# Query rounds over all head pairs, kept stacks of keys and queries, and low pieces by VectorE, in an attention and feed-forward kernel

## The chip, the cores and the metric

The kernel runs on one core of one Trainium2 chip. Its engines are TensorE (matmuls; PE in the profile, PEld for its weight loads), VectorE (DVE), ScalarE (ACT), GpSimd (POOL) and SyncE (SP), whose queue issues the DMAs. The metric is the device time of one execution in microseconds; less is better.

## The reference

Attention over 8 batches of 8 heads with 576 queries and keys of width 64, where all scores that lie more than `tau` below the greatest of their row are dropped, and a feed-forward part over the 4608 rows of the result. Cut to what is computed:

```python
def _attn_ref(q, k, v, tau):                       # q, k, v: 8 x 8 x 576 x 64
    scores = scale * np.matmul(q, k.transpose(0, 1, 3, 2))
    thresh = np.max(scores, axis=-1, keepdims=True) - tau
    scores = np.where(scores >= thresh, scores, -1000000000.0)
    attn = np.exp(scores - np.max(scores, axis=-1, keepdims=True))
    attn = attn / (np.sum(attn, axis=-1, keepdims=True) + 1e-09)
    return np.matmul(attn, v)

def _moe_ref(x, w_in, w_out, s, b):                # x: 4608 x 512
    h = x @ w_in                                   # 512 x 2048
    g = s * np.maximum(h, 0.0) ** 2 + b
    return g @ w_out                               # 2048 x 512
```

## The kernel before

Every product runs in half precision on pieces: a 32-bit number is scaled by a power of two and split into a high piece (its 16-bit value) and a low piece (what is left), and products of pieces are added up. Batch 0 alone is done in plain 32-bit form while the weights are loaded and split; batches 1 to 7 are "split".

**Order.** Nothing is written in the order in which it runs. `Plan.add` takes each operation with its engine, what it reads and writes and when it is wanted; `Plan.run` then sets every engine's order from these. Each engine, and SP's queue with the DMAs, takes its instructions in that order, one behind the other.

**Visits.** A visit is one head pair of a batch. In batches 1 to 7 (`WHOLE`) a visit goes over all 576 queries: nine score tiles, four of 128 queries for each head and one with the last 64 queries of both. `make_tiles` sets them, `Visit.load` loads raw q, k (`rq`, `rk`, two buffers) and v (`rv`, one), and `Visit.prepare` makes the pieces. It takes the greatest absolute values (VectorE, L401) and powers of two from them, then scales k and q in place (POOL, L420), casts to the high piece (ScalarE, L422), and subtracts for the low one (POOL, L423). DMAs (L430, L437) stack them for each head: 128 partitions with the high and low queries one above the other, so that one matmul adds two products of pieces. Two such pairs of stacks exist, in the buffers of four weights whose pieces have been moved away (`STACKS_IN`, `moved`). The last queries are copied by POOL (L439) to `qt16`, laid out so that both heads share one matmul. v is scaled (POOL, L448), cast (ScalarE, L458) and its low piece subtracted (POOL, L459), in three buffers.

**A score tile** (`split_tile`): scores on TensorE (L549; four matmuls of 288 columns, the tile of the last queries six) into one of two banks, `s` and `t`; the row maximum on VectorE (L553); threshold and scale on POOL and ScalarE (L555, L557); exponentials on ScalarE (L559); threshold and sum on VectorE (L561); its reciprocal (L564, L566); high piece on ScalarE (L567, L569); low piece on VectorE (L570); a transposing DMA into `ea` or `eb` (L575). When 256 or 320 queries of both heads are there, `with_v` multiplies with v (L585, 14 matmuls for each head, the heads in the two halves of the partitions) and ScalarE copies the result to `xb` (L592).

**Blocks.** 256 rows of the attention's result are a block of the feed-forward part, 512 values each, so all four head pairs must be through; the 64 last queries of four batches make a further one (a tail). `Block.stage` takes a maximum (VectorE, L760), finds powers of two and makes the block's pieces (ScalarE L778, VectorE L782). 16 steps follow, one for each 128 columns of the hidden layer: 12 matmuls `h` (L798), on ScalarE L802, L805, L806, on POOL `gl` (L807), six matmuls `o` (L813). VectorE finishes a block (L827) and SP writes it out (L832). In batch 0 the visits go in two rounds, queries 0 to 255 of all pairs and then the rest; in batches 1 to 7 both blocks of a batch become ready with its last visit.

## Time and profile before

| | |
|---|---|
| median of 3 runs | 1171.56 us (1170.17 to 1172.82) |
| the profiled execution's own time | 1172.21 us |
| its span, first to last instruction | 1170.4 us |
| mean granted TensorE clock | 0.992 |
| busy PE / PEld / DVE / ACT / POOL | 95 / 67 / 75 / 83 / 62% |

How to read it: the span is that of one execution under the hardware profiler. Busy time is the time in which an engine executes something, matmuls' ends are modelled, and instructions of an engine overlap a little, so that from the start of one to the start of the next is often shorter than the duration. The granted clock is a share of TensorE's full 2.4 GHz.

### The profile page before, as it was taken

What the parts mean: (1) busy time and instruction counts of PE and PEld (TensorE: products, weight loads), DVE (VectorE), ACT (ScalarE), POOL (GpSimd) and SP (SyncE); (2) the same over time, 40 slices, a digit from 0 to 9 for tenths busy, and PEclk for the clock granted to TensorE, in tenths of its full rate; (3) what the DMA queues carried; (4) which work ended last, traced back from release to release, by engine and by line L of the source; (5) the groups of instructions that cost most, each with busy time, mean ns of one, the idle gap of its engine ahead of it and who ended that gap; (6) DMA issues with size and microseconds to landing.
All of it is one profiled execution on the core that took longest, in us unless ns stands there. A gap on an engine that the chain in (4) does not pass through costs nothing.

```text
span 1170.4 us, 26444 instructions
## 1 busy us (share of the span) xinstructions
PE 1117.2 (95%) x8826; PEld 781.3 (67%) x8826; DVE 874.8 (75%) x1838; ACT 965.8 (83%) x2301; POOL 721.4 (62%) x1369
## 2 busy tenths in 40 slices
PE   8988888978999999999999999999999999999998
PEld 7766565746666676666676666766776766666665
DVE  5798888798988987888888888787888888730011
ACT  6997888978989889888898888888998989854443
POOL 5565586665767776776675667776777777522200
PEclk9999999998999999999999999999999999999999
DMA  5960168776878777886676777867778786700000
GB/s 163 351 224 2 38 127 165 155 155 146 146 162 153 160 153 149 150 165 132 133 148 139 138 147 145 166 138 144 151 153 172 138 160 127 132 26 1 19 19 18
DMA packets 362232, 155.37 MB, mean 133 GB/s; under 512 B 316016, under 2 KB 340592, under 8 KB 362096
## 3 DMA queue, kind: packets, MB, share of 16 engines
q1 hardware_dynamic: 362096, 153.69, 62.2%
q8 instruction: 69, 1.13, 0.4%
q14 instruction: 67, 0.55, 0.1%
HBM read 46.01 MB, written 9.44 MB: 47 GB/s over the span
## 4 chain that ended last, share of the span: by engine, by line
PE 61%; ACT 12%; DVE 8%; DMA 7%; issue 5%; POOL 4%; SPq 3%; DVEq 0%; POOLq 0%; ACTq 0%
PE h L798 23%; PE o L813 22%; PE pv L585 7%; PE s L549 4%; PE t L549 4%; ACT em L559 2%; ACT en L567 2%; DMA eb<-en 2%; DVE em L561 2%; DVE st L553 2%; DMA rv<-in_v_dram 1%; DMA ea<-in_q_dram 1%; DVE en L570 1%; POOL k L423 1%; ACT iw L802 1%
## 5 line engine op out<-in xcount | busy, mean ns | idle before, releaser
L798 PE MATMUL h<-xp,iw 128*128 128x256 f16 x3456 | 426.4, 273 | 12.9 <-ACT iw L802 8.2
L798 PEld LDWEIGHTS <-iw 128*128 128x128 f16 x3456 | 334.9, 98 | 100.8 <-issue 25.2
L807 POOL TENSOR_TENSOR gl<-iw,gh 128x256 f16<-128x256 f32 x272 | 195.9, 722 | 153.6 <-ACT gh L806 123.8
L813 PE MATMUL o<-ow,gh 128*128 128x512 f16 x864 | 256.9, 379 | 1.6 <-DVE iw L827 1.6
L570 DVE SCALAR_TENSOR_TENSOR en<-em,st,en 128x576 f16<-128x576 f32 x252 | 226.1, 901 | 24.1 <-ACT en L567 21.9
L567 ACT ACTIVATE en<-em,st 128x576 f16<-128x576 f32 x252 | 192.8, 769 | 25.6 <-DVE st L566 21.3
L802 ACT ACTIVATE iw<-h 128x256 f32<-128x256 f32 x288 | 109.0, 378 | 90.1 <-PE h L798 85.5
L813 PE MATMUL o<-ow,gl 128*128 128x512 f16 x432 | 163.7, 379 | 0.0
L555 POOL TENSOR_SCALAR st<-st,wz 128x1 f32<-128x1 f32 x252 | 121.5, 483 | 66.8 <-DVE st L553 48.3
L813 PEld LDWEIGHTS <-gh 128*128 128x128 f16 x1152 | 110.7, 98 | 77.7 <-issue 3.7
L805 ACT ACTIVATE iw<-iw 128x256 f32<-128x256 f32 x288 | 119.7, 416 | 4.0
L806 ACT CAST gh<-iw 128x256 f16<-128x256 f32 x288 | 115.9, 402 | 6.1 <-PE o L813 1.3
L564 POOL TENSOR_SCALAR st<-st 128x1 f32<-128x1 f32 x252 | 70.4, 279 | 81.6 <-DVE em L561 48.0
L561 DVE SCALAR_TENSOR_TENSOR em<-s,st,em 128x576 f32<-128x576 f32 x126 | 102.2, 811 | 21.2 <-ACT em L559 15.7
L549 PEld LDWEIGHTS <-ow 128*128 128x128 f16 x896 | 85.3, 98 | 48.4 <-issue 8.5
L561 DVE SCALAR_TENSOR_TENSOR em<-t,st,em 128x576 f32<-128x576 f32 x126 | 102.4, 813 | 14.4 <-ACT em L559 10.5
L585 PE MATMUL pv<-eb,v 128*64 128x256 f16 (+1 forms) x784 | 107.5, 289 | 5.2 <-DMA eb<-en 5.1
L585 PE MATMUL pv<-ea,v 128*64 128x256 f16 (+1 forms) x784 | 109.2, 290 | 1.3 <-DVE vs L407 1.3
L553 DVE TENSOR_REDUCE st<-s 128x1 f32<-128x576 f32 x126 | 94.5, 750 | 21.0 <-PE s L549 20.6
L585 PEld LDWEIGHTS <-v 128*64 128x64 f16 x1568 | 85.0, 110 | 33.2 <-issue 17.7
L559 ACT ACTIVATE em<-s,st,wz 128x576 f32<-128x576 f32 x126 | 104.0, 825 | 1.2
L559 ACT ACTIVATE em<-t,st,wz 128x576 f32<-128x576 f32 x126 | 104.0, 826 | 1.0
(198 smaller groups left out, 1840.1 us busy)
## 6 DMA issues: line engine op xcount, KB each, us to landing
ow<-k SPq DMA_DIRECT2D x112, 144.0 KB, 2.5
rk<-in_k_dram SPq DMA_DIRECT2D x29, 288.0 KB, 3.2
iw<-in_moe_w_in_dram SPq DMA_DIRECT2D x16, 512.0 KB, 9.4
ow<-in_moe_w_out_dram SPq DMA_DIRECT2D x16, 512.0 KB, 9.2
out_dram<-iw SPq DMA_DIRECT2D x32, 256.0 KB, 2.6
rq<-in_q_dram SPq DMA_DIRECT2D x28, 288.0 KB, 3.5
rv<-in_v_dram SPq DMA_DIRECT2D x56, 128.0 KB, 2.8
ow<-k SPq DMA_DIRECT2D x112, 64.0 KB, 2.2
```

The source lines that it names most:

```text
L549: nc.tensor.matmul(ps[:, hf], stat, kk, start=(n == 0), stop=(n == len(seq) - 1))
L555: pool((260, 263), lambda: nc.gpsimd.tensor_scalar(out=line, in0=top, scalar1=-1.0, scalar2=va.wz[:, 2:3], op0=ALU.mult, op1=ALU.add), [(k ...
L559: act((636, 740), lambda: nc.scalar.activation(out=halves, in_=ps, func=AF.Exp, bias=bias, scale=va.wz[:, 1:2]), [bk, (ks_, 4), (va.kwz, 1 ...
L561: dve((740, 900), lambda: nc.vector.scalar_tensor_tensor(out=halves, in0=ps, scalar=line, in1=halves, op0=ALU.is_ge, op1=ALU.mult, accum_o ...
L567: act((668, 774), lambda: nc.scalar.activation(out=pieces[:, 0:S], in_=ex, func=AF.Copy, scale=unit), [em_k, (ks_, 3)], [en_k], i)
L570: dve2((740, 825), lambda: nc.vector.scalar_tensor_tensor(out=pieces[:, S + T:2 * S + T], in0=ex, scalar=unit, in1=pieces[:, 0:S], op0=ALU ...
L585: nc.tensor.matmul(ps[j * D:(j + 1) * D], hd.v[:, (n + 1) % 5, u * D:(u + 1) * D], lazy[("ea", "eb")[j]][:, n, g.c0:g.c0 + g.n], start=(i ...
L798: nc.tensor.matmul(ps, wi[w][f][:, c * P:(c + 1) * P], x[:, u, c, :], start=(c == 0 and i == 0), stop=(c == NC - 1 and i == 2))
L802: act((357, 473), lambda: nc.scalar.activation(out=g(), in_=ps, func=AF.Relu, scale=H_DOWN), [h, (f"w{(0, 1, 5)[k3]}", "i", 2)], [kg], at)
L805: act((320, 417), lambda: nc.scalar.activation(out=g(), in_=g(), func=AF.Square), [kg], [kg], at)
L807: do((712, 735) if not self.last else (340, 425), lambda: eng.tensor_tensor(out=lo, in0=g(), in1=hi, op=ALU.subtract), [kg, f"gh{k3}"], [f ...
L813: nc.tensor.matmul(bank["o"][:, t, :], a[:, ts_], w, start=(f == 0 and i == 0), stop=(f == NF - 1 and i == 2))
```

## The change

Each of the batches 1 to 7 is now done like batch 0: first queries 0 to 255 of all four head pairs, four score tiles each, then queries 256 to 511 and the last 64, five tiles each. A pair's preparation is done once in a batch and what it makes is kept for the second round. So four visits have buffers of their own: eight stacks instead of four (one in the memory of the plain batch's `qs`, seven in weights' buffers, whose pieces are moved), eight buffers for v instead of three (six in weights' buffers), four of the small tables. The stacks now hold three things, the queries in full and both pieces of the keys, so that `qt16` goes. The tile of the last queries takes eight matmuls with 64 columns of the array each, alternating between the heads, which lie in the two halves of the partitions. High pieces are cast by ScalarE with the scale as part of the instruction, low pieces made by VectorE in one instruction (multiply by the scale, subtract the high piece); POOL's seven instructions of that kind go. A visit's stacks are made by four DMAs of 216 KB instead of eight of 144 and 64 KB. The columns of `ea` and `eb` are used in turn by even and odd pairs.

```diff
-WHOLE = range(1, 8)
...
-STACKS_IN = 6
+STACKS_IN = (None, 0, 7, 8, 9, 10, 11, 12)
+VALUES_IN = (1, 2, 3, 4, 5, 6)
+SPARES = (1, 2, 4, 5, 6, 3)
...
-            self.n, self.wz, self.kwz = i % 2, wz[i % 3], f"wz{i % 3}"
-            self.kpc = [("piece", self.n, c) for c in range(4)]
-            self.kqt = [(f"qt16_{self.n}", j) for j in range(2)]
+            self.n, self.m, self.wz, self.kwz = i % 4, i % 2, wz[i % 4], f"wz{i % 4}"
+            self.kpc = [("piece", self.m, c) for c in range(4)]
...
+        def stack(self, j):
+
+            return lazy["y", 2 * self.n + j]
...
             for c, (t, key) in enumerate(raw):
-                up = x[:, 9 + c:10 + c]
-                pool((722, 742), lambda t=t, up=up: nc.gpsimd.tensor_scalar(
-                    out=t, in0=t, scalar1=up, scalar2=1.0, op0=ALU.mult, op1=ALU.mult), [key, (kx, 3)], [key], at)
-                act((612, 717), lambda c=c, t=t: nc.scalar.copy(out=self.piece(2 * c), in_=t), [key], [self.kpc[2 * c]], at)
-                pool((1385, 1420), lambda c=c, t=t: nc.gpsimd.tensor_tensor(
-                    out=self.piece(2 * c + 1), in0=t, in1=self.piece(2 * c), op=ALU.subtract),
-                    [key, self.kpc[2 * c]], [self.kpc[2 * c + 1]], at)
+                up, hi, lo = x[:, 9 + c:10 + c], 1 - c, 2 + c
+                act((612, 717), lambda hi=hi, t=t, up=up: nc.scalar.activation(
+                    out=self.piece(hi), in_=t, func=AF.Copy, scale=up), [key, (kx, 3)], [self.kpc[hi]], at)
+                dve2((658, 743), lambda hi=hi, lo=lo, t=t, up=up: nc.vector.scalar_tensor_tensor(
+                    out=self.piece(lo), in0=t, scalar=up, in1=self.piece(hi), op0=ALU.mult, op1=ALU.subtract),
+                    [key, (kx, 3), self.kpc[hi]], [self.kpc[lo]], at)
             for j in range(2):
                 own = slice(j * D, (j + 1) * D)
                 for u in range(2):
-                    to = slice(u * D, (u + 1) * D)
-                    dma(144, lambda j=j, own=own, to=to: nc.sync.dma_start(
...
-                pool((330, 330), lambda j=j, own=own: nc.gpsimd.tensor_copy(
...
+                    to, turn = slice(u * D, (u + 1) * D), slice(4 * m, 4 * m + 3) if not u else slice(4 * m + 3, 4 * m, -1)
+                    dma(216, lambda j=j, own=own, to=to, turn=turn: nc.sync.dma_start(
+                        out=self.stack(j)[to], in_=lazy["k"][own, turn]), self.kpc[u:u + 3], [("y", 2 * n + j, u)], at)
...
-            pool((775, 796), lambda: nc.gpsimd.tensor_scalar(
-                out=flat, in0=flat, scalar1=x[:, 11:12], scalar2=1.0, op0=ALU.mult, op1=ALU.mult),
...
-                pool((775, 797), lambda t=t, own=own, other=other, j=j: nc.gpsimd.tensor_tensor(
-                    out=t[:, :, other], in0=rv[:, j], in1=t[:, :, own], op=ALU.subtract), kr + keys, keys, at)
...
+                dve2((400, 485), lambda hd=hd, own=own, other=other, j=j, up=up: nc.vector.scalar_tensor_tensor(
+                    out=hd.values()[:, :, other], in0=rv[:, j], scalar=up, in1=hd.values()[:, :, own], op0=ALU.mult, op1=ALU.subtract),
...
         def scores():
             for hf in range(2):
-                c, j = slice(hf * HS, (hf + 1) * HS), ti.slot
-                if j is None:
-                    seq = [(qt16[va.n][:, u], va.piece(w)[:, c]) for u, w in ((0, 0), (0, 1), (1, 0))]
-                else:
-                    seq = [(va.queries_of(j)[:, ti.n * P:(ti.n + 1) * P], va.keys_of(j, w)[:, c]) for w in range(2)]
-                for n, (stat, kk) in enumerate(seq):
-                    nc.tensor.matmul(ps[:, hf], stat, kk, start=(n == 0), stop=(n == len(seq) - 1))
+                c = slice(hf * HS, (hf + 1) * HS)
+                for w in (1, 2):
+                    for j in js:
+                        y = va.stack(j)
+                        to, q = (ps[:, hf], slice(ti.n * P, (ti.n + 1) * P)) if ti.slot is not None else (
+                            ps[j * T:(j + 1) * T, hf], slice(M, S))
+                        nc.tensor.matmul(to, y[:, 0, q], y[:, w, c], start=(w == 1), stop=(w == 2))
...
-    visits = []
-    for bi in range(B):
-        if bi in WHOLE:
-            visits += [(bi, p_, 0, NQ, True) for p_ in range(NP)]
-        for u in range(0 if bi in WHOLE else 2):
-            visits += [(bi, p_, 2 * u, 2 * u + 2, (bi > 0 and p_ < NP // 2) == (u == 0)) for p_ in range(NP)]
+    visits = [(bi, p_, 2 * u, 2 * u + 2, u == 1) for bi in range(B) for u in range(2) for p_ in range(NP)]
...
+        u, at = us[0], (0, M - NB + T)[pair % 2]
...
-        for j, n in [(0, 0), (0, 1), (0, 2), (1, 0), (1, 1), (0, 3), (None, 4), (1, 2), (1, 3)]:
+        for j, n in [(0, 0), (1, 0), (None, 2), (0, 1), (1, 1)]:
+            if j is None and not tail:
+                continue
```

On VectorE, around the staging of the third block, which is the first block of batch 1. L553, L561, L566 and L570 are the instructions of a score tile (`st` its statistics, `en` its pieces), L760 the maximum over a block, `x`, L401 that over raw `rk`, `rq` or `rv`, L412 a power of two for it, L827 the end of a block. Before:

```order
L553 TENSOR_REDUCE st_74<-t 128x1
L570 SCALAR_TENSOR_TENSOR en_77<-em_80,st_71,en_77 128x576
L566 RECIPROCAL st_73<-st_73 128x1
L412 TENSOR_SCALAR vs_103<-vs_103 128x3
L827 SCALAR_TENSOR_TENSOR iw_528<-o,power_96,iw_454 128x512
L570 SCALAR_TENSOR_TENSOR en_75<-em_78,st_72,en_75 128x576
L570 SCALAR_TENSOR_TENSOR en_76<-em_79,st_73,en_76 128x576
L760 TENSOR_REDUCE norm_84<-x_113 128x1
L561 SCALAR_TENSOR_TENSOR em_80,st_74<-t,st_74,em_80 128x576
L764 TENSOR_TENSOR nsq_86<-norm_84 128x1
```

and with the change, where the numbers of the lines are four to five lower (L549 is the maximum, L557 the threshold, L562 the reciprocal, L566 the low piece, L406 the maximum over raw values, L756 that over the block):

```order
L549 TENSOR_REDUCE st_70<-t 128x1
L566 SCALAR_TENSOR_TENSOR en_77<-em_80,st_74,en_77 128x576
L406 TENSOR_REDUCE vm_83<-rq 128x1
L566 SCALAR_TENSOR_TENSOR en_75<-em_78,st_69,en_75 128x576
L557 SCALAR_TENSOR_TENSOR em_79,st_70<-t,st_70,em_79 128x576
L549 TENSOR_REDUCE st_71<-s 128x1
L756 TENSOR_REDUCE norm_84<-x_113 128x1
L549 TENSOR_REDUCE st_72<-t 128x1
L760 TENSOR_TENSOR nsq_86<-norm_84 128x1
L557 SCALAR_TENSOR_TENSOR em_80,st_71<-s,st_71,em_80 128x576
L562 RECIPROCAL st_70<-st_70 128x1
```

The maximum over the block stood behind the low piece of the 35th of batch 1's 36 tiles; now it stands behind that of the 19th, and reductions over raw values of later visits stand near it.

On POOL, at the preparation of the first visit of batch 2. L555 and L564 are the small instructions of a tile. Before:

```order
L415 TENSOR_TENSOR vs_103<-vs_103,spread 128x3
L420 TENSOR_SCALAR rk<-rk,vs_103 128x576
L564 TENSOR_SCALAR st_73<-st_73 128x1
L420 TENSOR_SCALAR rq<-rq,vs_103 128x576
L423 TENSOR_TENSOR k<-rk,k 128x576
L423 TENSOR_TENSOR k<-rq,k 128x576
L555 TENSOR_SCALAR st_74<-st_74,wz_92 128x1
L442 TENSOR_SCALAR wz_90<-vs_103 128x1
L445 TENSOR_SCALAR wz_90<-vs_103,spread 128x1
L448 TENSOR_SCALAR rv<-rv,vs_103 128x640
```

and with the change (L551, L560 the small ones of a tile, L803 the feed-forward's `gl`, L420 and L436 to L442 a visit's small tables, L714, L764 and L767 a block's powers of two), at the same preparation:

```order
L560 TENSOR_SCALAR st_72<-st_72 128x1
L803 TENSOR_TENSOR gl_120<-iw_393,gh_117 128x256
L714 TENSOR_SCALAR power_94<-power_94 128x1
L551 TENSOR_SCALAR st_73<-st_73,wz_91 128x1
L420 TENSOR_TENSOR vs_102<-vs_102,spread 128x3
L439 TENSOR_SCALAR wz_90<-vs_102,spread 128x1
L551 TENSOR_SCALAR st_74<-st_74,wz_91 128x1
L764 TENSOR_SCALAR power_94<-power_94 128x1
L767 TENSOR_TENSOR power_94<-power_94 128x1
L560 TENSOR_SCALAR st_73<-st_73 128x1
```

The wide instructions on `rk`, `rq`, `rv` and `k`, which stood ahead of a tile's small ones, are gone; only the visit's tables are left.

On VectorE, in the first round of batch 2 with the change (L427 makes a low piece of q or k, L452 one of v, whose buffers now lie in those of the weights, `ow`):

```order
L562 RECIPROCAL st_74<-st_74 128x1
L427 SCALAR_TENSOR_TENSOR k<-rk,vs_103,k 128x576
L549 TENSOR_REDUCE st_70<-t 128x1
L566 SCALAR_TENSOR_TENSOR en_77<-em_80,st_74,en_77 128x576
L557 SCALAR_TENSOR_TENSOR em_78,st_69<-s,st_69,em_78 128x576
L452 SCALAR_TENSOR_TENSOR ow_304<-rv,vs_103,ow_304 128x5x64
L452 SCALAR_TENSOR_TENSOR ow_376<-rv,vs_103,ow_376 128x5x64
L562 RECIPROCAL st_69<-st_69 128x1
L557 SCALAR_TENSOR_TENSOR em_79,st_70<-t,st_70,em_79 128x576
L427 SCALAR_TENSOR_TENSOR k<-rq,vs_103,k 128x576
```

Before, the rows between the tiles of the same place read:

```order
L570 SCALAR_TENSOR_TENSOR en_75<-em_78,st_69,en_75 128x576
L570 SCALAR_TENSOR_TENSOR en_76<-em_79,st_70,en_76 128x576
L561 SCALAR_TENSOR_TENSOR em_80,st_71<-s,st_71,em_80 128x576
L401 TENSOR_REDUCE vm_82<-rk 128x1
L553 TENSOR_REDUCE st_72<-t 128x1
L760 TENSOR_REDUCE norm_85<-x_111 128x1
L566 RECIPROCAL st_71<-st_71 128x1
L553 TENSOR_REDUCE st_73<-s 128x1
L561 SCALAR_TENSOR_TENSOR em_78,st_72<-t,st_72,em_78 128x576
L401 TENSOR_REDUCE vm_82<-rq 128x1
```

Four low pieces of a visit have come in between the tiles' instructions.

## Rows read from the trace of the kernel before

**Rows 1.** The page: busy time and share of the span of TensorE.
```profile
PE 1117.2 (95%) x8826; PEld 781.3 (67%) x8826; DVE 874.8 (75%) x1838; ACT 965.8 (83%) x2301; POOL 721.4 (62%) x1369
```
**Rows 2.** Busy us (instructions) of PE, PEld, DVE, ACT, POOL; clock, DMA share, GB/s.
```profile
300.00:360.00 60.00, 57.49 (x464) 39.45 (x462) 49.84 (x102) 52.33 (x129) 41.43 (x79) 1.00 0.77 153
...
480.00:540.00 60.00, 59.26 (x478) 41.64 (x478) 52.84 (x113) 53.48 (x133) 39.83 (x77) 1.00 0.77 150
...
900.00:960.00 60.00, 60.00 (x473) 41.47 (x473) 53.15 (x112) 54.07 (x134) 44.05 (x78) 1.00 0.78 152
...
1040.00:1080.00 40.00, 39.48 (x277) 26.94 (x276) 3.28 (x4) 20.21 (x50) 10.48 (x17) 1.00 0.04 14
```
**Rows 3.** The same in stretches of 10 us.
```profile
140.00:150.00 10.00, 8.06 (x53) 4.88 (x52) 5.57 (x10) 4.83 (x13) 9.09 (x16) 1.00 0.61 158
...
160.00:170.00 10.00, 8.13 (x55) 5.21 (x54) 9.38 (x19) 8.75 (x20) 9.22 (x17) 1.00 0.56 114
...
250.00:260.00 10.00, 5.89 (x50) 3.23 (x47) 10.00 (x21) 7.98 (x18) 7.34 (x11) 1.00 0.78 147
260.00:270.00 10.00, 4.24 (x18) 2.49 (x19) 8.24 (x18) 4.50 (x9) 6.09 (x18) 0.52 0.83 163
270.00:280.00 10.00, 10.00 (x76) 6.74 (x75) 7.79 (x14) 7.80 (x21) 3.83 (x9) 0.80 0.65 154
```
**Rows 4.** The chain of waits from 245 to 285 us: start us, us, what.
```profile
258.37 1.78 POOL k L423
...
261.49 2.01 DMA ow<-k
...
267.08 1.30 DVE xp L782
```
**Rows 5.** Timeline of PE: start us, us, line, out<-in, partitions x columns.
```profile
562.62 0.65 PE L549 MATMUL s<-ow 128*128 128x288 f16 x4
563.11 0.59 PE L813 MATMUL o<-ow,gh 128*128 128x512 f16 x2
...
909.78 0.65 PE L549 MATMUL s<-ow 128*128 128x288 f16 x4
910.37 0.32 PE L585 MATMUL pv<-ea,v 128*64 128x320 f16 x1
...
912.16 0.30 PE L585 MATMUL pv<-eb,v 128*64 128x320 f16 x1
912.39 1.48 PE L798 MATMUL h<-xp,iw 128*128 128x256 f16 x12
```
**Rows 6.** Timeline of DVE, five instructions without a gap.
```profile
561.16 0.82 DVE L561 SCALAR_TENSOR_TENSOR em<-s,st,em 128x576 f32<-128x576 f32 x1 [1.19 <-ACT em L559]
...
561.90 0.81 DVE L570 SCALAR_TENSOR_TENSOR en<-em,st,en 128x576 f16<-128x576 f32 x1
562.63 0.75 DVE L553 TENSOR_REDUCE st<-t 128x1 f32<-128x576 f32 x1
563.31 0.76 DVE L553 TENSOR_REDUCE st<-s 128x1 f32<-128x576 f32 x1
563.99 0.15 DVE L566 RECIPROCAL st<-st 128x1 f32<-128x1 f32 x1
```
**Rows 7.** Groups of instructions: busy us, mean ns of one, idle before.
```profile
L570 DVE SCALAR_TENSOR_TENSOR en<-em,st,en 128x576 f16<-128x576 f32 x252 | 226.1, 901 | 24.1 <-ACT en L567 21.9 <-DMA eb<-en 0.4
...
L459 POOL TENSOR_TENSOR v<-rv,v 128x320 f16<-128x320 f32 x56 | 45.0, 804 | 16.5 <-ACT v L458 15.3
...
L827 DVE SCALAR_TENSOR_TENSOR iw<-o,power,iw 128x512 f32<-128x512 f32 (+1 forms) x40 | 28.9, 743 | 12.6 <-PE o L813 12.6
...
L782 DVE SCALAR_TENSOR_TENSOR xp<-x,power,xp 128x1024 f16<-128x1024 f32 x16 | 21.6, 1348 | 38.7 <-ACT xp L778 38.5
...
L760 DVE TENSOR_REDUCE norm<-x 128x1 f32<-128x1024 f32 x16 | 19.4, 1211 | 5.0 <-ACT x L592 5.0
L439 POOL COPY qt<-k 64x128 f16<-64x128 f16 x56 | 19.2, 343 | 2.0
```

More of the change, by code (lines that the diff above doesn't have):

```diff
@@ L685, in weight_scales @@
         pool((1800, 1800), back, ["wpower", "s_", "b"], ["wback"], at + 1)
-    moved = [(STACKS_IN + n, 1) for n in range(4)]
+    moved = [(f, 1) for f in STACKS_IN if f is not None]
     def pieces_of_weights(f, at):
@@ L900, in make_tiles @@
             if j is not None:
[L901 to L903 removed]
+                ti.heads, ti.parts = [(A, Bh)[j]], [(("ea", "eb")[j], at + n * P, fl)]
             else:
[L905 removed]
+                ti.heads, ti.parts = [A, Bh], [("ea", NB, slice(0, T)), ("eb", NB, slice(T, P))]
             tiles.append(ti)
+        tiles[-1].end = [group]
@@ L907, in make_tiles @@
         if pair == NP - 1:
-            blocks = tiles[-1].blocks
-            blocks += [("full", bi, u) for u in us]
-            if t1 == 4 and bi % 4 == 3:
-                blocks.insert(0 if bi == B - 1 else len(blocks), ("tail", bi // 4, 0))
+            tiles[-1].blocks = [("full", bi, u)]
+            if u and bi % 4 == 3:
+                tiles[-1].blocks.insert(0 if bi == B - 1 else 1, ("tail", bi // 4, 0))
         return tiles
     pairs = [Plain(0, p_) for p_ in range(NP)]
-    heads = [Head(2 * vi + j, vis[0], 2 * vis[1] + j) for vi, vis in enumerate(visits) for j in range(2)]
```

110 lines of the change are left out of this document (53 added, 57 removed).

## Prediction

> **What bounds the kernel now.** I read the busy times first. TensorE is at work for 1117 of 1170 us [rows 1], and the 10 us and 60 us stretches show where it is not. In the steady part it leaves 2.5 us of 60 idle at 300, 0.7 at 480 and none at 900, with VectorE at 50 to 53 of 60 [rows 2]. At the end, where only the feed-forward part is left, 277 matmuls take 40 us; a step is 12 + 6 of them, so a step costs 2.60 us [rows 2]. So the span is TensorE's own work plus the holes in it. One hole is large: from 250 to 280 us TensorE is busy 5.9, 4.2 and 10.0 us of the slices, and the granted clock reads 0.52 and 0.80 in the last two, which is most of the time at 1.2 GHz instead of 2.4 after the engine had stood still [rows 3]. The chain of waits tells why. Both blocks of batch 0 are used up, those of batch 1 become ready only when the whole batch is through, and just then the next visit is prepared: POOL's subtractions, the stack DMA, then VectorE's low piece of the staged block, for which the h matmuls wait [rows 4]. The prologue has smaller gaps, 1.9 us at 140 and 1.9 at 160 [rows 3].
>
> I write "tile" for 128 queries of one head, or the 64 last queries of both, against 576 keys; each batch from 1 to 7 has 36, before and after. The sum is made against the profiled execution's own 1172.2 us (span 1170.4, the rest around it); the median of the runs, 1171.6, lies 0.65 below it, and I subtract that at the end.
>
> **1. Rounds: blocks become ready half a batch earlier.** After the change the first block of a batch is complete after 16 tiles instead of 36. In the order, VectorE takes the maximum of the third block (the first of batch 1) behind 35 tiles' low pieces before, and behind 19 now, when TensorE has 30 of the 32 steps of batch 0 behind it. Two steps (5.2 us) and the score tiles between them then cover the staging. So the hole should be filled. Its price: idle 4.1 us, then 10 - 4.24 x 0.52 = 7.8, then 10 x 0.20 = 2.0, together 13.9; an ordinary stretch at 300 has 2.5 of 60 idle anyway, 1.2 of 30, so **-12.7 us** is the gain, with 0 as the other end, if the hole only moves. The end of the program keeps its form: TensorE alone at 2.60 us a step.
>
> **2. The tile of the last queries.** 28 times six matmuls of 288 columns become eight, each 64 columns of the array wide, in pairs that write the two halves of the partitions. A score tile of four matmuls takes 0.49 us from its start to the next matmul (562.62 to 563.11) [rows 5], so 0.12 each, six 0.73. If a pair runs side by side, eight cost four, 0.49. The product with v shows that pairs do: its 14 pairs, 320 columns wide, take 2.02 us (910.37 to 912.39), 0.144 a pair, where one after the other they would take twice that [rows 5]. But the same rows show what the change of form costs. The score tile ahead of such a group takes 0.59 instead of 0.49, and its last pair 0.23 instead of 0.13: 0.10 us going in, 0.10 coming out. So a tile costs 0.49 + 0.20 = 0.69 against 0.73, and 28 of them give **-1.1 us**; the ends are -6.7 (no cost of the change of form) and +6.7 (pairs one after the other). I take the middle since these rows have the same form.
> The Trainium skill, "TensorEngine Tiling (Array Packing)", section "Key Properties", says that changing the tiling mode drains the engine. The 0.10 us on either side agrees; without that rule the term would be -6.7, with it -1.1.
>
> **3. Work leaves POOL.** Seven groups of POOL go, from the low pieces of v, 45.0 us, to the copies of the last queries, 19.2: 218 us in all, 7.8 per visit [rows 7] (the first and the last of the seven stand there). POOL is 62% busy and mostly off the path, so most of this is worth nothing. In two places it ends last: in the hole (already counted), and ahead of the first split tile at 147 us. The gaps of TensorE there are 1.9 and 1.9 us [rows 3]; I take half, **-2 us**, with 0 and -3.8 as ends. The stacks' eight DMAs per visit become four of 216 KB each; they are issued on SP's queue, ahead of the transposes, and the queue gets shorter. The visit's own loads are the same. The high pieces on ScalarE are the same two casts with a scale in them. I cost all this at nothing: its cover is that a stack is now asked for once in a batch and stays.
>
> **4. VectorE takes the low pieces.** Per visit two 576 wide ones of the form of L570, and two 320 wide. L570 runs 0.81 us undisturbed, with the next instruction 0.73 behind it, and 0.90 in the mean [rows 6, 7], so one occupies 0.73 to 0.82; 320 columns by proportion 0.41 to 0.46. I take 0.80 and 0.45, an estimate from those rows: 2.5 us a visit, 70 us in all on an engine that is busy 875.
> What matters is where. A tile costs VectorE 0.74 (L561) + 0.82 (L570) + 0.68 (L553) + 0.15 (L566) = 2.39 us [rows 6]. A visit's preparation costs three reductions at 0.7, small ones some 0.4 and the new 2.5: 5.0. A block costs 1.2 + 1.35 to stage and twice 0.74 to finish, 4.0 [rows 7]. A first round has 16 tiles and, if nothing moved, all four preparations: 38.2 + 20.0 + 4.0 = 62.2 us. TensorE has in it 16 steps, 16 tiles at 0.49 and four products of 1.6 (2.02 by 256/320): 41.6 + 7.8 + 6.5 = 55.9. The second round is the other way about: 51.8 against 60.4. So a first round would be bound by VectorE by 6.3 us, 44 us over seven batches. The order moves part of the preparation into the second round before. Counting its rows at these prices in stretches of nine tiles, VectorE has more to do than TensorE in eight stretches from tile 18 on: by 4.4, 3.1, 2.5, 3.8 and 3.0 us in five, under 1 in three, 18.7 in all, and each is followed by one with 2 to 8 us to spare (without the change the same count gives 13.2, of which 6.7 is the hole). In-order queues with two score banks can make up part of that. So the bounds are 0 and 44; I take a third of 18.7, **+6 us**, nearer to 0, because VectorE runs at 53.15 of 60 at 900 us with TensorE never idle [rows 2]. Behind a late VectorE instruction wait the score matmuls, since their bank is not free, and behind those the feed-forward matmuls in TensorE's queue.
> The Trainium skill, "SBUF — State Buffer", section "Who interferes with whom", says that a VectorE instruction with two SBUF inputs and a GpSimd instruction that reads SBUF exclude each other for their whole length. L570's mean of 0.90 against 0.81 agrees. By it the 30% that POOL loses would give VectorE some 30% of 252 x 0.09, 7 us, over the program, and the term would be nearer to 4 than to 6.
>
> **Sum.** 1172.2 - 12.7 - 1.1 - 2 + 6 = 1162.4; less 0.65, **1162 us**.
>
> **Rivals.**
> *VectorE becomes the bound.* Place: the first rounds of batches 2 to 5, and the two batches before, where all three engines are even. From tile 18 to 90 the counts give VectorE 232 us and TensorE 236. If VectorE cannot go above 53.15 of 60, the most that any row here shows, those 232 take 262, while TensorE with its usual 2% idle would take 240: +22, and 8 more in the later batches (3.8 + 3.0 + 0.6 + 0.8), so +30: 1172.2 - 15.8 + 30 - 0.65 = **1186**. It decides from +15.8 on. For it speaks that the order stages each block with only one or two steps left, so there is little stock; against it that feed-forward steps need no VectorE.
> *All of it works.* VectorE's surplus is absorbed, the pairs cost no change of form, the prologue's gaps close: 1172.2 - 12.7 - 6.7 - 3.8 - 0.65 = **1148**. The row at 900 us speaks for the first, the rows of the product with v against the second.
> *The hole only moves.* Four visits are prepared in the first 16 tiles of batch 1, so that block may be late and batch 0's steps run out as before: 1172.2 - 1.1 - 2 + 6 - 0.65 = **1174**. Against it stand the two steps in hand.
>
> **How the numbers follow.** Forecast 0.48 (1155 to 1169), all of it works 0.24, VectorE the bound 0.18, the hole moves 0.10. A measurement of this kernel tells 0.2% (2.3 us) from no change. Faster: all but the edge of the forecast, and the second rival, 0.70; same 0.08, from the edge of the forecast and half of the last rival; slower 0.22. The range goes from 1147, the second rival, to 1181, most of the way to the first; below and above lie about 0.2.
>
> **What would show it.** Right: no stretch with a granted clock under 0.9 between 240 and 290 us; the third block staged near 200 us; the tail tile's eight matmuls within 0.7 us; VectorE at 54 or more of 60 around 280 to 420 us with TensorE at 58 or more. Wrong: TensorE waiting for score banks that VectorE frees, in the first halves of the batches, by more than 15 us in all; or feed-forward matmuls waiting for staged pieces again.

## The result, and the profile after

The changed kernel takes 1136.74 us in the median (1134.79 to 1137.64, 4 runs) beside 1172.19 for the kernel before in the same session: a ratio of 0.969 (95% interval 0.967 to 0.972), 35.4 us less. The forecast was 1162 with a range of 1147 to 1181: faster was right, but the time lies 10 us below the range and the gain is three and a half times the one worked out. One run of a kernel below, e8, went at a granted clock of 0.851 and took 1274.0 us; its time in the table is the median of the other three.

The span and the busy line of the page after (beside [rows 1]):

```profile
span 1135.8 us, 26196 instructions
PE 1106.7 (97%) x8882; PEld 770.5 (68%) x8882; DVE 917.3 (81%) x1950; ACT 967.7 (85%) x2301; POOL 546.5 (48%) x1117
```

POOL is busy 175 us less than before, VectorE 42.5 us more, and TensorE stands still for 29 us of the span instead of 53. The place is found with four long stretches: ahead of the old hole, around it, and the two halves of the steady part. Columns: stretch and its length, busy us and instructions of PE, PEld, DVE, ACT, POOL, then granted clock, DMA share, GB/s. Before:

```profile
0.00:240.00 240.00, 215.25 (x1770) 160.29 (x1771) 196.62 (x420) 205.56 (x436) 151.14 (x304) 0.99 0.59 153
240.00:300.00 60.00, 49.08 (x375) 32.70 (x374) 52.86 (x110) 49.16 (x117) 37.45 (x72) 0.89 0.74 150
300.00:660.00 360.00, 350.95 (x2812) 243.39 (x2810) 301.07 (x629) 318.56 (x781) 252.78 (x473) 1.00 0.76 149
660.00:1040.00 380.00, 377.14 (x3023) 261.64 (x3021) 307.97 (x654) 333.70 (x824) 257.38 (x486) 1.00 0.71 141
```

and after:

```profile
0.00:240.00 240.00, 222.70 (x1833) 164.66 (x1834) 200.94 (x434) 209.48 (x442) 131.67 (x274) 1.00 0.60 157
240.00:300.00 60.00, 59.52 (x487) 40.76 (x485) 56.04 (x121) 54.29 (x134) 32.77 (x64) 1.00 0.84 162
300.00:660.00 360.00, 354.55 (x2866) 243.80 (x2865) 319.04 (x677) 322.85 (x793) 179.92 (x371) 1.00 0.73 147
660.00:1040.00 380.00, 379.49 (x3091) 261.63 (x3090) 324.54 (x686) 337.68 (x828) 187.24 (x383) 1.00 0.74 142
```

From such rows I work out what a stretch **loses**: the time in which PE is idle, plus PE's busy time times what the clock lacks. The hole's stretch loses 60 - 49.08 + 49.08 x 0.11 = 16.3 us before and 0.5 after. In the same way 0 to 240 us goes from 26.9 to 17.3 (the clock's two digits make that uncertain by 1 us; added up from rows of 10 us, the first two losses before are 26.1 and 15.0), and 300 to 1040 from 11.9 to 6.0. Together 55.1 against 23.7: 31.4 of the 35.4 us. Of the other 4 the tail tile has 1.1 (below); the rest I can't place. Over all kernels below, the profiled execution's time less its loss is 1114 to 1121 us, so the losses carry the times to within some 4 us.

The five 10 us stretches that answer [rows 3], three of them shown, are full, where before they had 8.1, 8.1, 5.9, 4.2 and 10.0 us busy, and the 60 us stretches that answer [rows 2] hold a surprise:

```profile
140.00:150.00 10.00, 10.00 (x67) 6.21 (x65) 5.71 (x10) 7.68 (x16) 6.42 (x13) 1.00 0.58 137
160.00:170.00 10.00, 10.00 (x63) 5.81 (x61) 8.02 (x15) 8.40 (x19) 5.28 (x11) 1.00 0.93 210
260.00:270.00 10.00, 10.00 (x86) 6.86 (x85) 8.65 (x20) 9.33 (x23) 6.25 (x14) 1.00 0.55 110
...
300.00:360.00 60.00, 58.76 (x484) 40.76 (x483) 55.34 (x119) 54.74 (x134) 32.82 (x64) 1.00 0.80 159
660.00:720.00 60.00, 60.00 (x502) 41.82 (x502) 56.91 (x120) 53.96 (x132) 31.21 (x64) 1.00 0.90 183
1040.00:1080.00 40.00, 39.55 (x272) 26.35 (x271) 5.83 (x14) 20.57 (x50) 12.83 (x23) 1.00 0.04 14
```

At 660 us VectorE is busy 56.91 of 60 while TensorE never stops; before, the highest was 53.15 [rows 2], which the prediction took for a possible ceiling. At the end, from 1040 us on, TensorE is as full as before.

### The profile page after: what moved, and what is told of

Its sections match the earlier page's. It is cut to its first block, busy times and chain, and to the rows that moved or that the text cites. A ratio compares the mean times of both kernels' runs of the same rounds, so it can differ in the third digit from the quotient of the medians.

```text
span 1135.8 us, 26196 instructions
## 1 busy us (share of the span) xinstructions
PE 1106.7 (97%) x8882; PEld 770.5 (68%) x8882; DVE 917.3 (81%) x1950; ACT 967.7 (85%) x2301; POOL 546.5 (48%) x1117
## 4 chain that ended last, share of the span: by engine, by line
PE 74%; ACT 8%; DVE 6%; issue 3%; DMA 3%; POOL 1%; SPq 1%; DVEq 0%; ACTq 0%; POOLq 0%
PE h L794 27%; PE o L809 27%; PE pv L581 7%; PE s L545 4%; PE t L545 4%; ACT en L563 2%; ACT em L555 1%; DVE em L557 1%; DMA eb<-en 1%; PE pv L517 1%; DVE st L549 1%; ACT iw L798 1%; DMA ea<-en 1%; PE t L504 1%; PE s L481 1%
## 5 line engine op out<-in xcount | busy, mean ns | idle before, releaser
L794 PE MATMUL h<-xp,iw 128*128 128x256 f16 x3456 | 424.8, 273 | 10.2 <-ACT iw L798 9.4
L803 POOL TENSOR_TENSOR gl<-iw,gh 128x256 f16<-128x256 f32 x272 | 202.3, 744 | 208.4 <-issue 82.6
L566 DVE SCALAR_TENSOR_TENSOR en<-em,st,en 128x576 f16<-128x576 f32 x252 | 209.6, 836 | 21.4 <-ACT en L563 20.1
L809 PE MATMUL o<-ow,gh 128*128 128x512 f16 x648 | 192.9, 379 | 0.7 <-DVE iw L823 0.7
L551 POOL TENSOR_SCALAR st<-st,wz 128x1 f32<-128x1 f32 x252 | 121.5, 483 | 111.3 <-DVE st L549 68.0
L560 POOL TENSOR_SCALAR st<-st 128x1 f32<-128x1 f32 x252 | 86.1, 342 | 144.1 <-DVE em L557 76.2
L809 PE MATMUL o<-iw,gh 128*128 128x512 f16 x504 | 150.0, 379 | 0.2 <-DVE iw L823 0.2
L809 PE MATMUL o<-ow,gl 128*128 128x512 f16 x324 | 122.8, 379 | 0.0
L557 DVE SCALAR_TENSOR_TENSOR em<-t,st,em 128x576 f32<-128x576 f32 x126 | 102.3, 812 | 19.9 <-ACT em L555 13.6
L545 PEld LDWEIGHTS <-ow 128*128 128x128 f16 (+1 forms) x980 | 85.1, 100 | 47.8 <-issue 13.5
L557 DVE SCALAR_TENSOR_TENSOR em<-s,st,em 128x576 f32<-128x576 f32 x126 | 102.3, 812 | 13.0 <-ACT em L555 8.9
L555 ACT ACTIVATE em<-s,st,wz 128x576 f32<-128x576 f32 x126 | 103.9, 824 | 1.1
L555 ACT ACTIVATE em<-t,st,wz 128x576 f32<-128x576 f32 x126 | 103.8, 824 | 1.1
L553 ACT ACTIVATE st<-st,wz 128x1 f32<-128x1 f32 x252 | 72.9, 290 | 36.3 <-DVE st L549 34.8
L809 PEld LDWEIGHTS <-gl 128*128 128x128 f16 x576 | 56.3, 98 | 68.0
L549 DVE TENSOR_REDUCE st<-t 128x1 f32<-128x576 f32 x126 | 94.4, 749 | 8.8 <-PE t L545 7.2
```

The lines of the kernel that those rows point to most:

```text
L545: nc.tensor.matmul(to, y[:, 0, q], y[:, w, c], start=(w == 1), stop=(w == 2))
L551: pool((260, 263), lambda: nc.gpsimd.tensor_scalar(out=line, in0=top, scalar1=-1.0, scalar2=va.wz[:, 2:3], op0=ALU.mult, op1=ALU.add), [(k ...
L555: act((636, 740), lambda: nc.scalar.activation(out=halves, in_=ps, func=AF.Exp, bias=bias, scale=va.wz[:, 1:2]), [bk, (ks_, 4), (va.kwz, 1 ...
L557: dve((740, 900), lambda: nc.vector.scalar_tensor_tensor(out=halves, in0=ps, scalar=line, in1=halves, op0=ALU.is_ge, op1=ALU.mult, accum_o ...
L566: dve2((740, 825), lambda: nc.vector.scalar_tensor_tensor(out=pieces[:, S + T:2 * S + T], in0=ex, scalar=unit, in1=pieces[:, 0:S], op0=ALU ...
L794: nc.tensor.matmul(ps, wi[w][f][:, c * P:(c + 1) * P], x[:, u, c, :], start=(c == 0 and i == 0), stop=(c == NC - 1 and i == 2))
```

## The experiments

Eighteen kernels ran. The kernel before took 1170.8 to 1173.5 us in their sessions. "Order" in the table is a number that the planner assumes for the time from one engine to another, 150 ns in both kernels; 152 changes no instruction, only the order.

| kernel | rounds in 1 to 7 | low pieces of q, k, v | order | us | loses 0:300 | 300:1040 |
|---|---|---|---|---|---|---|
| before | no | POOL | 150 | 1172.2 | 43.2 | 11.9 |
| e7_before_152 | no | POOL | 152 | 1178.7 | 42.4 | 14.0 |
| e4_before_dve | no | VectorE | 150 | 1168.7 | 40.5 | 9.6 |
| e9_neither | no | POOL | 150 | 1155.4 | 34.0 | 4.5 |
| e14_neither_152 | no | POOL | 152 | 1166.7 | 37.1 | 10.1 |
| e1_whole | no | VectorE | 150 | 1160.6 | 37.6 | 6.9 |
| e15_whole_152 | no | VectorE | 152 | 1155.7 | 32.7 | 8.8 |
| e2_pool | yes | POOL | 150 | 1148.0 | 20.3 | 9.7 |
| e16_pool_152 | yes | POOL | 152 | 1145.6 | 19.7 | 9.9 |
| after | yes | VectorE | 150 | 1136.7 | 17.8 | 6.0 |
| e8_after_152 | yes | VectorE | 152 | 1138.2 | 17.7 | 6.1 |

**How much an order alone does.** One number of the planner, in both kernels:

```diff
-    HANDOVER = 150
+    HANDOVER = 152
```

> The kernel before with the same number of the planner moved from 150 to 152: the same instructions in a slightly different order. If the order's chance is small: within 3 us of 1172. If the kernel before had a bad order by chance: 10 us or more faster.

> The changed kernel with one number of the planner moved from 150 to 152: the same instructions in a slightly different order. It measures how much of any difference is chance of the order. If the order's chance is small: within 3 us of 1137. If the gain of 35 us is largely chance: 10 us or more away.

Measured 1178.66 (ratio to before 1.0048, 1.0031 to 1.0066; before took 1173.23 in that session) and 1138.19 (0.9705, 0.9689 to 0.9721; two expectations below take 1139.0, +2.3, the median of all four runs). With the pairs that follow, the same work in two orders differs by +5.4, +1.5, +11.3, -4.9, -2.3 and -2.1 us, some 6 us in the root mean square. The runs of one kernel agree to about 2 us; it is the order that is uncertain. So a comparison of two kernels whose order differs is good to no better than 6 us, one of two means over both orders to some 4, and what follows rests on both orders wherever it can.

**Rounds and VectorE's pieces, each without the other.** e1 sets a pair's two rounds back to back, nearly as one visit does in the kernel before (the first block of a batch is asked for with the 31st of its 36 tiles, there with the 36th); e2 has POOL scale and subtract again; e9 does both.

```diff
 e1: visits
+ [... batch 0 as it is] + [(bi, p_, 2 * u, 2 * u + 2, u == 1)
+     for bi in range(1, B) for p_ in range(NP) for u in range(2)]
 e2: prepare, q and k (v alike)
+ pool(..., nc.gpsimd.tensor_scalar(out=t, in0=t, scalar1=up, scalar2=1.0, ...))
+ act(..., nc.scalar.copy(out=self.piece(hi), in_=t))
+ pool(..., nc.gpsimd.tensor_tensor(out=self.piece(lo), in0=t, in1=self.piece(hi), op=ALU.subtract))
```

> The changed kernel with its two rounds of a head pair back to back in batches 1 to 7, so that both blocks of a batch become ready with the last pair again; stacks, pieces and the tile of the last queries stay as changed. Theory A (three parts: blocks ready earlier some 15 us, the prologue some 10, the rest of the program some 10 by the work that left POOL): only the first part goes, about 1152 us, with the hole and a low granted clock back near 250 to 280 us. Theory B (the rounds bring nearly all): 1165 us or more, with TensorE behind in the later batches too. Theory C (blocks ready earlier matter little): about 1137.

> The changed kernel with scaling and low pieces of q, k and v on POOL as before (rounds, kept stacks, last queries in halves stay). Theory A: the rest of the program loses its some 10 us, about 1147, with POOL near 700 us busy and VectorE near 850. Theory of the prediction (VectorE's load costs about 6 us): faster than the changed kernel, about 1131. Theory B (the rounds bring nearly all): 1137 within 3.

> The changed kernel with both of its main parts taken back: a pair's two rounds stand back to back in batches 1 to 7, and POOL again scales and subtracts; the kept stacks, four copies, tail tile and their order stay. Rounds alone taken back gave 1160.6, POOL alone 1147.9. Theory A, the two parts add up: 1136.7 + 23.9 + 11.2 = 1172 us. Theory B, VectorE's relief is worth as little without rounds as in the kernel before (4.8): 1165 us. Either way TensorE's work done by 220 us should be some 8 us ahead of the kernel before if the prologue's gain belongs to what is left.

> The run without rounds and with POOL's pieces (1155.4 us), with the planner's assumed time from engine to engine at 152 ns instead of 150: the same work in another order, which moved the kernel before by +5.3 and the changed one by +2.3 us. Theory A, that rounds and VectorE's pieces help each other is real: 1152 to 1159 us, and below the run with VectorE at 152. Theory B, the 1155.4 was a lucky order: 1160 us or more.

> The run without rounds and with VectorE's pieces (1160.6 us) at 152 ns. Theory A, without rounds VectorE's pieces cost time: 1158 to 1165 us, at least 3 above the same with POOL. Theory B, that was the order: at or below the same with POOL.

> The run with rounds and POOL's pieces (1147.9 us) at 152 ns. Theory A, with rounds VectorE's pieces are worth 11 us: 1147 to 1152 us, at least 8 above the changed kernel at 152 ns (1139.0). Theory B, part of the 11 was the order: 1140 to 1145 us.

Beside what was expected: e1 (1160.6) lies between its A and B, e2 (1148.0) fits A, e9 (1155.4) lies under both of its theories, e14 and e15 fit B, e16 (1145.6) ends just above B's range. At 150 the table looks like a strong interplay: VectorE's pieces gain 11.2 us with rounds and cost 5.2 without. The second order takes that back: there they gain 7.4 with rounds and 11.0 without, since e9's 1155.4 was a lucky order (e14: 1166.7). What stands in the means of both orders: rounds bring 14.3 us with POOL's pieces and 20.7 with VectorE's; VectorE's pieces bring 9.3 with rounds, and 2.9 without, which 4 us of uncertainty can't tell from nothing; and what is left of the change when both are taken back brings 14.4 (1175.4 to 1161.1).

The hole is the one place where all orders agree. Rows of 240 to 300 us, of e1, e15, e9, e2 and e16 in turn:

```profile
240.00:300.00 60.00, 46.97 (x361) 31.59 (x360) 55.16 (x122) 50.06 (x115) 28.91 (x61) 0.87 0.80 160
240.00:300.00 60.00, 54.44 (x421) 36.20 (x420) 55.09 (x120) 52.42 (x128) 30.55 (x67) 0.97 0.73 156
240.00:300.00 60.00, 52.75 (x426) 35.38 (x424) 55.28 (x116) 52.19 (x125) 40.51 (x78) 0.97 0.73 157
240.00:300.00 60.00, 57.77 (x458) 38.22 (x457) 50.33 (x112) 54.93 (x138) 43.54 (x85) 1.00 0.88 168
240.00:300.00 60.00, 58.39 (x487) 40.02 (x482) 52.23 (x113) 54.97 (x138) 43.22 (x81) 1.00 0.85 152
```

In the first three TensorE is idle for 5.6 to 13 us and the granted clock falls; with rounds, in the last two, it is idle for 1.6 to 2.2 us at the full clock, whoever makes the pieces. Up to 300 us all kernels of the table without rounds lose 33 to 43 us, those with rounds in all batches 18 to 20.

**Rounds in batches 0 and 1 only.**

```diff
+ [... for bi in range(2) for u in range(2) for p_ in range(NP)] +
+ [... for bi in range(2, B) for p_ in range(NP) for u in range(2)]
```

> The changed kernel with rounds in batches 0 and 1 only; in batches 2 to 7 a pair's rounds stand back to back. Rounds in all batches are worth 23.9 us (1160.6 without). Theory A, most of that is the hole at 250 to 280 us, which rounds in batch 1 alone fill, and the rest (some 8 us) comes from blocks that are ready in time later: 1143 to 1148 us, no granted clock below 0.9 from 240 to 300 us. Theory B, all of it is the hole: 1137 us. Theory C, the hole moves to the next batch, where the blocks again come late: 1152 us or more, with a gap of over 5 us between 300 and 420 us.

Measured 1152.97 (0.9833, 0.9817 to 0.9848). In time it fits C, by the trace A: from 240 to 300 us TensorE is busy 59.34 at a clock of 1.00, and no gap comes in the next batch. The time was lost earlier, 25.5 us by 240 us instead of 17.3, with one wait of 3.6 us for a stack's DMA in 120 to 180 us; from 300 to 1040 us it loses 10.2, 3 more than e1. So rounds in batch 1 are enough for the hole, and they fill it rather than move it. Whether later rounds bring anything can't be told from one order.

**VectorE's load.** e4 is the kernel before with the pieces made by VectorE as in the change. e3 is the changed kernel in which VectorE makes the low pieces of q and k twice, with the same result.

```diff
 e4, prepare of the kernel before: the change's own lines for act(...) and dve2(...) in place of POOL's
 e3, prepare of the changed kernel
                 dve2((658, 743), lambda ...: nc.vector.scalar_tensor_tensor(out=self.piece(lo), ...
+                dve2((658, 743), lambda ...: nc.vector.scalar_tensor_tensor(out=self.piece(lo), ...
```

> The kernel before, with only the low pieces of q, k and v moved to VectorE and their scaling into ScalarE's casts. Theory A: some 10 us faster than before, about 1162, the hole at 250 to 280 us stays or shrinks by POOL's 3 us in the chain. Theory of the prediction: no faster than 1168, VectorE's load eats it. Theory B: 1172 within 3.

> The changed kernel with every low piece of q and k made twice, by two like VectorE instructions: 56 more of 576 columns, some 45 us more work on VectorE (the second writes the same values). Theory that VectorE is absorbed while it stays under some 95% of a stretch: 1137 to 1142. Theory of the prediction (VectorE's surplus in the first rounds is a third felt): about 1137 + 15 = 1152. If VectorE is the bound in the first rounds already: the whole 45, about 1180.

e4 took 1168.72 (0.9954, 0.9938 to 0.9969), 4.8 us under the kernel before in its session and within an order's chance; e3 1147.71 (0.9785, 0.9771 to 0.9800), between "absorbed" and a third felt. In e3 VectorE has 37.5 us more to do (954.8 against 917.3) and the kernel is 11.0 us slower, some 0.3 us for each. That is nearly twice what an order alone does in the mean, though one pair of orders differs as much (11.3). So load on VectorE seems to cost time; one order can't settle how much. A row of e3 shows how full it can be while TensorE runs on:

```profile
250.00:260.00 10.00, 10.00 (x88) 7.05 (x86) 10.00 (x26) 9.33 (x24) 6.32 (x13) 1.00 0.86 188
```

And yet with rounds it pays to move the pieces from POOL to VectorE. The groups over the whole program, of e2 and of after, then of e16 and of e8, the same pair in the other order, show a relief:

```profile
L567 DVE SCALAR_TENSOR_TENSOR en<-em,st,en 128x576 f16<-128x576 f32 x252 | 225.6, 900 | 23.1 <-ACT en L564 20.9
```

```profile
L566 DVE SCALAR_TENSOR_TENSOR en<-em,st,en 128x576 f16<-128x576 f32 x252 | 209.6, 836 | 21.4 <-ACT en L563 20.1
```

```profile
L567 DVE SCALAR_TENSOR_TENSOR en<-em,st,en 128x576 f16<-128x576 f32 x252 | 220.1, 876 | 26.6 <-ACT en L564 24.8
```

```profile
L566 DVE SCALAR_TENSOR_TENSOR en<-em,st,en 128x576 f16<-128x576 f32 x252 | 208.0, 828 | 20.7 <-ACT en L563 18.8
```

The low piece of a tile takes 836 ns instead of 900 and 828 instead of 876, 16 and 12 us over the program. So it is in every kernel here: 828 to 841 ns where VectorE makes the pieces of q, k and v, 876 to 923 where POOL does. In both orders the steady part then loses 3.8 us less with rounds (9.7 to 6.0, 9.9 to 6.1). What goes there are TensorE's waits for the transposed pieces of a tile and for a visit's stacks, both of which stand behind low pieces. Waits from 300 to 1040 us (us in all, times, longest), of e2 and of e16:

```profile
PE s L546 <- DMA ow<-k: 2.2, 3, 1.3
...
PE pv L582 <- DMA eb<-en: 1.2, 2, 1.0
...
PE pv L582 <- DMA ea<-en: 0.4, 1, 0.4
```

```profile
PE pv L582 <- DMA eb<-en: 3.8, 1, 3.8
...
PE t L546 <- DMA ow<-k: 1.2, 1, 1.2
```

3.8 and 5.0 us in all. In the changed kernel no such wait is left, in e8 one of 0.2. That earlier low pieces cause this is argued; a shorter wait of VectorE for POOL's small instructions can't be it, since it falls in one order only (for the reciprocal from 14.4 to 6.1 us, e2 to after, but 9.9 to 10.3, e16 to e8).

**The stretch ahead of the hole.** The weights' loads stand earlier in the new order: the first leaves SP's queue at 8.74 us instead of 21.98, and the first `h` matmul starts at 103.2 us instead of 110.7. e5 moves only these loads, by 13 us, in the kernel before. e12 tells the planner that they are 20 us more urgent, and it sets every engine's order anew.

```diff
 e5: -        self.order = sorted((s, n) ...
     +        self.order = sorted((s - (13000 if n in self.early else 0), n) ...
 e12: in place(), the weights' loads come 20000 ns earlier among what is wanted
```

> The kernel before, with nothing changed but the place of the weights' loads in SyncE's queue: they stand as if wanted 13 us earlier, ahead of the loads of later head pairs. Theory A (the prologue's gain comes from weights that arrive earlier): the first feed-forward matmul near 103 us instead of 111, and 5 to 9 us faster, 1163 to 1167. Rival (the prologue is bound by VectorE and ScalarE whatever the loads do): 1172 within 2, or slower if the head pairs' data come late.

> The kernel before, where the planner is told that the weights' loads are 20 us more urgent and sets every engine's order anew from that (the first load then stands at place 15 of SP's queue instead of 26, and the first feed-forward step earlier in TensorE's order, as in the changed kernel). Theory A, the prologue's gain in the changed kernel is the earlier weights, ordered throughout: TensorE is 7 to 10 us ahead of the kernel before at 220 us, and the time is 1162 to 1167 us. Theory B, the gain needs the new buffers, and earlier weights only delay the first tiles, as when the loads alone were moved: 1175 to 1183 us.

e5 took 1183.01 (1.0078, 1.0055 to 1.0101), with 39.2 us lost by 240 us instead of 26.9: loads alone gain nothing. e12 took 1172.18 (0.9995, 0.9981 to 1.0009), neither A nor B. Its rows show why:

```profile
0.00:240.00 240.00, 219.27 (x1789) 162.04 (x1790) 193.17 (x411) 206.28 (x438) 152.69 (x301) 0.99 0.57 151
240.00:300.00 60.00, 46.85 (x354) 30.96 (x353) 53.47 (x115) 48.52 (x113) 39.19 (x74) 0.86 0.79 156
```

Up to 240 us it loses 22.9 instead of 26.9, but in the hole 19.7 instead of 16.3. What TensorE gains ahead of the hole it stands still for in it, since without rounds the third block comes when batch 1's attention is nearly through, however far the rest is. Its pieces, which ended the wait in [rows 4] at 267.08 us before, are made by VectorE in e12, e15 and the changed kernel at

```profile
269.19 1.28 DVE L784 SCALAR_TENSOR_TENSOR xp<-x,power,xp 128x1024 f16<-128x1024 f32 x1
```

```profile
259.27 1.28 DVE L778 SCALAR_TENSOR_TENSOR xp<-x,power,xp 128x1024 f16<-128x1024 f32 x1
```

```profile
227.92 1.28 DVE L778 SCALAR_TENSOR_TENSOR xp<-x,power,xp 128x1024 f16<-128x1024 f32 x1
```

Over the 13 kernels without rounds in batch 1, that time and the loss up to 300 us go together, some 1 us for each (from 259.27 and 32.7 in e15 to 280.69 and 55.0 in e5; the correlation is 0.96, and 0.87 without e5). How the loss is shared between the time ahead of 240 us and the hole differs: e1 has 18.5 and 19.1, e15 25.5 and 7.2.

**What is left: stacks, copies, tail tile, order.** e10 and e13 have two copies of a visit's stacks and of its table `vs` instead of four, without rounds, with VectorE's and with POOL's pieces; the eight buffers of v are counted by head and the tables `wz` apart, so the edit leaves these as they are, other than the two expectations say. e17 and e18 (order 152) are e9 with eight DMAs for a visit's stacks and POOL's copies of the last queries put back (what they copy isn't read, but the tail tile waits for them). e6 issues the tail tile's matmuls head by head.

```diff
 e10, e13: -  self.n, ... = i % 4, ...
           +  self.n, ... = i % 2, ...
 e17, e18: -  dma(216, ... out=self.stack(j)[to], ...)
           +  dma(144, ... out=self.stack(j)[to, 1:3], ...); dma(72, ... out=self.stack(j)[to, 0], ...)
           +  pool((330, 330), ... nc.gpsimd.tensor_copy(out=qt16[m][own, :, ...], ...))
 e6:       -  for w in (1, 2):
           -      for j in js:
           +  for j in js:
           +      for w in (1, 2):
```

> The changed kernel with a pair's rounds back to back in batches 1 to 7, and with two copies of a visit's stacks, v pieces and tables instead of four. Theory A, the prologue's gain (some 15 us of TensorE's work by 220 us in the run with four copies) has nothing to do with the copies: 1157 to 1165 us, as with four (1160.6), and the 15 us stay. Theory B, the four copies bring it, because the first four visits can be prepared early: the 15 fall to under 5, and the time is 1168 to 1175.

> The changed kernel without rounds in batches 1 to 7, with POOL's scaling and subtractions (1155.4 us, 17 under the kernel before), and with two copies of a visit's stacks, v pieces and tables instead of four. What is left of the change are the stacks of three parts made by four DMAs, no copies of the last queries, the tail tile, and the order that follows. Theory A, the 17 us come with these and not with the copies: 1151 to 1160 us. Theory B, the four copies bring them, since POOL's slow preparation can begin earlier: 1165 to 1173 us.

> The run without rounds and with POOL's pieces (1155.4 us), and with two more things of the kernel before put back: each visit's stacks made by eight DMAs (144 and 72 KB) instead of four of 216 KB, and POOL's two copies of the last queries per visit, for which the tail tile waits (what they copy is not read). Theory A, the 15 us that this kernel gains on the kernel before in the mean of two orders come from the shorter queue and the missing copies: 1168 us or more, and the mean of this run and the same at 152 ns is 1172 to 1178. Theory B, they come from elsewhere (the order of tiles, where the buffers lie): mean 1158 to 1166, as without the change (1161.1).

> The same with the planner's assumed time from engine to engine at 152 ns, since one order alone can be 5 us off either way. Beside 1166.7 without the change. Theory A: 1172 us or more. Theory B: 1160 to 1169.

> The changed kernel with the tile of the last queries' eight matmuls in another order: four for one head, then four for the other, so that neighbours write the same half of the partitions. If pairs in the two halves run side by side, each of the 28 tiles gets longer by up to 4 x 0.12 = 0.48 us: up to 13 us, about 1150. If they did not overlap before: 1137.

e10: 1160.93 beside 1160.6 with four copies; e13: 1153.73 beside 1155.4. Without rounds two more copies of the stacks show no gain; v's buffers were not tested. e17: 1164.74, e18: 1162.67, in the mean 1163.7 beside 1161.1: the eight DMAs and POOL's copies cost 2.6 us, within the chance of an order. e6: 1135.84 beside 1136.74; not because pairs didn't overlap before, as its expectation has it, but because they overlap in e6 too (last section). So of the 14.4 us that are left, copies of the stacks, the number of DMAs and POOL's copies seem to carry little. By the losses the 14.4 lie ahead of 300 us (42.8 to 35.6 in the mean of both orders) and after it (13.0 to 7.3). Ahead of 300 the third block's pieces come 3.0 us earlier in the mean (268.2 to 265.2 us). What brings that and the rest (the order of tiles within a visit, the first block of a batch being asked for five tiles earlier, v's buffers, where the buffers lie, or the order that the planner finds for them) stays open.

The tail tile could be read directly, in one of 28 before and one after; the first two rows are an ordinary `h` and what follows it, before:

```profile
560.18 1.47 PE L798 MATMUL h<-xp,iw 128*128 128x256 f16 x12
561.49 0.65 PE L549 MATMUL t<-ow 128*128 128x288 f16 x4
...
311.29 0.90 PE L549 MATMUL t<-k,qt 128*128 128x288 f16 x6
312.03 0.59 PE L813 MATMUL o<-iw,gh 128*128 128x512 f16 x2
```

```profile
361.18 1.47 PE L794 MATMUL h<-xp,iw 128*128 128x256 f16 x12
362.58 0.68 PE L545 MATMUL s<-ow 128*64 128x288 f16 x8
363.19 0.61 PE L809 MATMUL o<-ow,gh 128*128 128x512 f16 x2
```

Six took 0.74 us to the next matmul, eight take 0.61, and the `h` ahead of them 1.40 instead of 1.31: 0.70 with both changes of form, where 0.69 was predicted from [rows 5]. 28 times 0.04 is 1.1 us.

## Why the prediction was wrong

By edits, in the means of both orders, forecast and runs compare so: rounds -12.7, measured -14.3 (with POOL's pieces); low pieces to VectorE, terms 3 and 4 together, +4, measured -9.3 (with rounds); everything else -1.1, measured -14.4 (without rounds only). The rounds were priced nearly right. Two steps failed: term 4, which has the sign of VectorE's pieces wrong, and "I cost all this at nothing" in term 3, which stands for 13 us. By places:

**The hole (-12.7): right in mechanism, too small in reach.** The third block's maximum moved from 260.69 to 218.64 us and the clock stayed at 1.00. In its own stretch the gain is 15.8 us (14.5 by rows of 10 us). What failed is that the hole was priced by itself. Up to 300 us the program is one stage: without rounds a gain ahead of the hole is lost again in it (e12), with rounds it stays. In that stage the loss went from 43.2 to 17.8 us, 25.4, where terms 1 and 3 together had 14.7; rounds alone take 15.6 of it (35.6 to 20.0 with POOL's pieces, in the mean of both orders).

**The tail tile (-1.1): right**, 0.70 us where 0.69 was worked out, and the middle value was the one to take. The Trainium skill, "TensorEngine Tiling (Array Packing)", section "Key Properties", has TensorE drain when its tiling mode changes; the 1.40 us instead of 1.31 ahead of the eight matmuls agrees with it.

**POOL and the prologue (-2, ends 0 and -3.8): too small.** The gaps at 140 and 160 us closed as expected, but the stretch to 240 us lost 9.6 us less. The step that failed is "I cost all this at nothing": only the edits' own instructions were costed, not that the planner sets the whole prologue anew, weights and feed-forward steps included. In the variants of the changed kernel without rounds the same stretch loses 17.8 to 26.0 us, so part of this is the chance of an order. That SP's shorter queue is worth nothing is not refuted: e17 and e18 show 2.6 us, which an order's chance covers.

**VectorE's pieces (+6): the sign was wrong.** Measured is a gain of 9.3 us with rounds, 11.2 in one order and 7.4 in the other. The load was sized somewhat too large: VectorE's busy time rose by 42.5 us, and with the 16.5 that tiles' low pieces gave back the new instructions added some 59, where 70 were taken. The relief was mis-sized. Low pieces of tiles fell from 901 [rows 7] to 836 ns, 16 us, where the prediction counted 7 and took them only into a side sentence. And term 4 looked for score matmuls that wait for VectorE, 0.7 us in the steady part after; it left out the waits for transposes and stacks, 3.8 and 5.0 us in the two orders with POOL's pieces and 0 and 0.2 with VectorE's, though term 3 had POOL as "mostly off the path". The Trainium skill, "SBUF — State Buffer", section "Who interferes with whom", lets VectorE's instructions with two SBUF inputs and GpSimd's reads exclude each other; the 900 and 836 ns of e2 and after, and the 876 and 828 of e16 and e8, agree with it.

**The steady part, which no term held.** "An ordinary stretch at 300 has 2.5 of 60 idle anyway" was taken to remain. From 300 to 1040 us the loss halved, 11.9 to 6.0. The largest waits of TensorE in this part, before and after (us in all, times, longest):

```profile
PE pv L585 <- DMA eb<-en: 3.2, 3, 1.7
PE h L798 <- ACT iw L802: 2.0, 2, 1.2
PE h L798 <- DVE xp L782: 1.4, 3, 0.7
```

```profile
PE h L794 <- ACT iw L798: 2.9, 4, 1.4
PE o L809 <- DVE iw L823: 0.9, 3, 0.4
```

The waits for the transposed pieces are gone, in the other order too (2.7 us to 0.2). Those for staged blocks are gone in this order only (1.4 to none; 0.4 to 0.7 at 152). Terms 2 and 4 had this part at +4.9.

**The rivals.** "VectorE becomes the bound" is refuted: its ceiling of 53.15 of 60 was only the highest row seen, and 56.91 and, for 10 us, 10.00 occur beside a TensorE that never stops. "All of it works" was nearest (1148), for a partly wrong reason, since the pairs do pay the change of form. The signs on the list came true (VectorE 55.34 and TensorE 58.76 at 300 us, score matmuls waiting for VectorE 0.7 us from 300 us on), but for the third block, which was staged at 219 to 228 us and not "near 200". Still the time was off: the list held only what the terms held.

No version here beats the changed kernel by more than an order's chance.

## What to carry to other kernels

Where a planner sets the order, run the same work in two or three orders before reading anything from a difference of under 1%: here a change of 2 ns in an assumed cost moved times by up to 11 us, and one pair of runs showed an interplay that the second order took back. Price a hole together with the stage ahead of it: here time gained ahead of the hole was given back in it, and stayed gained once the hole was filled. When work moves from one engine to another, count what other engines' instructions that shared time with the moved ones get back, and what comes earlier for it: here the same low piece took 876 to 923 ns beside POOL's wide instructions and 828 to 841 without them.
